# Attention into a token and channel mixer: v times the decay weights on VectorE, loads paced five deep, and a reordered start

## The chip, the cores and the metric

The kernel runs on one core of one Trainium2 chip. The metric is the device time of one execution in microseconds; the time before is the median of three runs. A profile is one execution recorded by the hardware profiler, with the kernel's line numbers as L followed by a number. The engines are TensorE (PE for the matmuls, PEld for the weight loads beside them), VectorE (DVE), ScalarE (ACT), GpSimd (POOL) and SyncE (SP). POOL and SP also issue the DMAs.

## The reference

Eight batches, eight heads, 576 positions, 64 channels per head. Attention with a decay that the input s gives, and behind it a mixer over tokens and over channels:

```python
cum  = np.cumsum(np.maximum(s, 0.0), axis=-1)
bias = -(cum[:, :, :, None] - cum[:, :, None, :])
scores = np.where(causal, -1e9, scale * q @ k.T + np.minimum(bias, 0.0))
attn = softmax(scores)
x    = (attn @ v) as (B, S, H * D)                # 8 x 576 x 512
u    = x + (relu(x.T @ w_tok1) @ w_tok2).T        # mixer over tokens
out  = u + relu(u @ w_ch1) @ w_ch2                # mixer over channels, 512 -> 1536 -> 512
```

## The kernel before, in words

**Decay.** The bias of a pair of positions is a difference of two cumulated sums, so the factor that belongs to the key can be put on v. The kernel scans s on DVE (cum, L534), takes exp(cum - cum_last/2) on ACT (wn, L540), turns it on PE (L560) into wT (L564) and multiplies v by it: vp = vf times wT (L631), with wT itself as a 65th column (L640, L642) that gives the denominator. Only two neighbouring blocks of 128 keys are taken for each block of queries. What that leaves out, and whether q and k are small enough to do without a maximum, is tested at the end: sums of squares of all q and k (`squares`, L657, on ACT at L647 into junk) and gaps in the weights make a flag, and if it is set a general path computes everything again. It isn't set for these inputs.

**Work of a batch.** `stage_qk` loads k and q of four heads (qkn, a ring of five buffers, cast to bfloat16 in the DMA, L462), `stage_v` loads v in five pieces (vf, two buffers, L613) and `merge_v` multiplies (vp, one buffer for even and one for odd batches). `quad` turns q and k of four heads on PE (L689) and evacuates them (kT, qT, L699 on ACT, L701 on DVE); `pair` computes scores (L731), exponentials on ACT (L739), the causal mask on DVE (L748, L756; in batch 0 instead a preset of -2048 that PE adds, L722), E times v (L802), reciprocals (L831) and the normalisation (L835). `tok` is the token mixer (L899, L961, L968), after which u must be turned: from batch 2 on by DMA transposes on SP into uT (L977). `chan` is the channel mixer (L1017, relu at L1024 or L1026, L1042, sum at L1050, store at L1055).

**What sets the order.** No order is written out by hand. Each operation is given to a planner (`Plan.op`) with the engines that may do it, its cost on each, what it reads and writes, and a priority. `Plan.run` simulates the engines by these costs and emits the instructions in the order of the simulated start times; each engine then works through its own instructions in that order, and waits in it for what an instruction needs. Loads are planned on one line of DMA time that begins at `dma_free` (6.0), each with a cost of its own (1.45 for a q or k load, 1.15 for a piece of v, 1.6, 0.3, 1.5, 0.4 for the token weights, 1.9 for a quarter of w_ch1 or w_ch2) and 0.9 for landing. A load that the plan has landing after 50 (`STEADY`) is given 2.0 more (`MARGIN_DMA`) before its users are planned. `lock=True` keeps two operations of DVE and POOL from running at the same time in the plan. Until planned time 45, PE's gaps are filled with matmuls on zeros (L1135).

**Loads.** All loads but four are issued by POOL, in one chain (`load_op`). The plan lets a load start only when the load eight before it has landed (`sent[-8]`). The order is: k and q of (0, 4), that is batch 0 from head 4 on; v of batch 0; the token weights; w_ch1; k and q of (1, 0); half of w_ch2; (1, 4); the other half; v of batch 1; then for each batch from 2 to 7 k and q of its first four heads, v, k and q of its other four; and at the very end once more k and q of batches 0 and 1, for their squares alone (`stage_sq`). The first k and q, s and one piece of v come over SP.

**Products.** v times wT is on DVE in batch 0, on DVE or POOL in batch 1, and on POOL from batch 2 on; POOL therefore issues loads and multiplies in turn, in its planned order.

Of the kernel before, what the change touches and what calls it, by code (L numbers as in the profile page):

```python
# [12 lines left out]


SWITCH = 0.095
STEADY = 50.0
# [38 lines left out]
class Plan:  # L55
# [11 lines left out]
    def op(self, alts, reads=(), writes=(), prio=0, dma=0.0, holds=(), after=None, mode=0, lock=False, alone=None):  # L67
        o = Op()
        o.alts = alts
        o.prio = prio  # L70
        o.dma = dma
        o.mode = mode
        o.lock = lock
        o.alone = alone
        o.idx = len(self.ops)
        o.deps = set()
        o.users = []
        o.bufs = []
# [24 lines left out]
        self.ops.append(o)  # L103
        return o

    def run(self, eps=0.03):
# [11 lines left out]
        for o in ops:  # L118
            if o.nd == 0:
                for e in o.alts:  # L120
                    cands[e].append(o)
        dma_free = 6.0
        mode = 0
# [19 lines left out]
        while left:  # L143
# [68 lines left out]
            for u in o.users:  # L212
# [155 lines left out]
def kernel(  # L368
# [18 lines left out]
    NJ = 5  # L387
# [63 lines left out]

    def load_op(fn, key, us, occ=0.75, prio=-1):

# [6 lines left out]
    def load_cast(n, b, h, i, src):  # L460
        def load():
            nc.gpsimd.dma_start(  # L462
                out=n.t[:, i, :, :],
                in_=src[b, h : h + 4, :, :].rearrange("(f e) (p r) d -> (e p) f (r d)", e=2, r=R))
        load_op(load, [(n, i)], 1.45, prio=-1 if b or h else -3)

# [49 lines left out]
    for ti, src in enumerate((k, q)):  # L516
# [4 lines left out]
        for f in range(2):  # L521
# [11 lines left out]
         reads=["s"], writes=["sr"], prio=-1)  # L533
    P.op({"DVE": (1.3, 1.6, lambda: nc.vector.tensor_tensor_scan(  # L534
        out=cum[:, :], data0=one_sb[:, :], data1=s_sb[:, :], initial=0.0, op0=ALU.mult, op1=ALU.add))},
        reads=["sr"], writes=["cum"], prio=-1)
    P.op(dve(1, lambda: nc.vector.tensor_scalar(
# [61 lines left out]
    def stage_v(b, cs=tuple(range(NJ))):  # L599
# [4 lines left out]
        for c in cs:  # L604
# [13 lines left out]
            load_op(load, [(vf, c)], 1.15 * n / 128, 0.92)  # L618
        if b:
            merge_v(b, cs)  # L620

    def merge_v(b, cs=tuple(range(NJ))):
        vf, vp = vbuf[b]
        odd = b % 2
        for c in cs:
# [3 lines left out]
            def mul(eng, c=c, n=n, p0=p0):  # L629
# [3 lines left out]
                    in1=wT[p0 : p0 + n, cw, b * H : b * H + H].unsqueeze(2).to_broadcast([n, H, D]), op=ALU.mult)  # L633
            alts = {} if b == 0 else {"POOL": (*c_pool(512, 0.0019), lambda mul=mul: mul(nc.gpsimd))}
            if b < 2:
                alts["DVE"] = (*c_dve(512), lambda mul=mul: mul(nc.vector))
            P.op(alts, reads=[(vf, c), "wT"], writes=[(vp, c)], prio=-2 if b < 3 else b * 10 + 5, lock=True)

        def ones(eng):
            eng.tensor_copy(out=vp.t[:, 0 : NJ - 1, :, D], in_=wT[:, 0 : NJ - 1, b * H : b * H + H])  # L640
            p0, cw = (64, NJ) if odd else (0, NJ - 1)
            eng.tensor_copy(out=vp.t[p0 : p0 + 64, NJ - 1, :, D], in_=wT[p0 : p0 + 64, cw, b * H : b * H + H])  # L642
# [29 lines left out]
    def quad(b, h):  # L672
# [4 lines left out]
        for ti in range(2):  # L677
# [6 lines left out]
            def tr(ti=ti, pv=pv):  # L684
                for r in range(R):
                    for e in range(2):
                        p0 = e * PR
                        for f in range(2):
                            nc.tensor.transpose(out=pv(e)[f * D : f * D + D, r * PR : (r + 1) * PR],  # L689
                                                in_=nat.t[p0 : p0 + PR, ti, f, r * D : (r + 1) * D],  # L690
                                                identity=ident[p0 : p0 + PR, p0 : p0 + PR])
            P.op({"PE": (R * 0.031, R * 0.031 + 0.21, tr)}, reads=([(nat, ti, 0), (nat, ti, 1)] if b == 0 and h == 0 else [(nat, ti)]) + ["ident"] + pads,
                 writes=[(pts[e], e) for e in range(2)], holds=[d[ti] for d in dsts], prio=(np_ - 30 * (b < 1 and h < 1), 2), mode=1)
            for e in range(2):
# [12 lines left out]
    def pair(b, h, kT, qT):  # L707
# [3 lines left out]
        for pc, piece in enumerate(PIECES):  # L711
# [7 lines left out]
            if b == 0:  # L719
                def preset(ps=ps, pc=pc):  # L720
                    for hh in range(2):
                        nc.tensor.matmul(out=ps.t[:, hh * 512 : hh * 512 + 512], lhsT=ident[:, :], rhs=neg[:, pc, :],  # L722
                                         start=True, stop=False)
                P.op({"PE": (2 * c_pe(512)[0], 2 * c_pe(512)[0] + 0.21, preset)}, reads=["neg", "ident"],
                     writes=[(ps, 0)], prio=(np_ - 9, 0))
# [115 lines left out]
    def load_w(fn, key, us, occ=0.75):  # L841
        load_op(lambda: nc.gpsimd.dma_start(**fn()), [key], us, occ)

# [240 lines left out]
    stage_v(1)  # L1084
    for b in range(2, B):
        stage_qk(b, 0)
        stage_v(b)
        stage_qk(b, 4)
    for b in range(2):
        for h in range(0, H, 4):  # L1090
            stage_sq(b, h)
    for b in range(B):
        for h in range(0, H, 4):
            quad(b, h)
        st = tok(b)
        chan(b, *st)

    P.op({"DVE": (1.3, 1.6, lambda: nc.vector.tensor_tensor_scan(
# [85 lines left out]
```

## Time and profile before

| | |
|---|---|
| median of three runs | 304.92 us (304.0 to 306.28) |
| the profiled execution | 306.06 us |
| its span | 304.3 us |
| granted TensorE clock, mean | 0.995 |
| DVE busy, 0 to 60 / 60 to 100 / 100 to 180 us | 40.23 / 29.90 / 46.23 us |
| POOL busy in the same stretches | 43.41 / 27.63 / 26.38 us |
| moved by DMA | 39.29 MB, on the queue of POOL 24.25 MB |

A row of the waits reads: who waited, for whom, microseconds in total, times, longest. A row of the timeline or of the chain begins with the start and the length in microseconds. A row of one line or tile gives the count and least, median and largest duration in nanoseconds, the first and last start, and the shapes. A row of a table of stretches gives the stretch, its length, busy time (and instructions) of the engines in the order PE, PEld, DVE, ACT, POOL, or of one group of instructions on the engines that have it, and then the granted clock, the mean share of the DMA engines and GB/s. DMA_DIRECT2D and DMA_TRANSPOSE rows show the issuing, not the transfer. "Issue" stands for time in which an engine waited for nothing that the profile shows.

### The profile page before, as it was taken

How to read it: one execution, taken by the hardware profiler on the slowest of the kernel's cores; microseconds unless marked ns; L12 is line 12 of the kernel's file. 1: busy time of each engine (PE TensorE's matmuls, PEld its weight loads, DVE VectorE, ACT ScalarE, POOL GpSimd, SP SyncE). 2: the span in 40 equal slices, each digit the busy share in tenths (PEclk: the TensorE clock that was granted, in tenths of full speed). 3: DMA queues.
4: the chain of work that ended last, by engine and by line, in shares of the span. 5: the costliest groups of instructions: out<-in, count | busy, mean ns of one | idle time of the engine just before them, and what ended most of it. 6: DMA issues, size and time to landing. Idle time of an engine off the chain costs nothing.

```text
span 304.3 us, 8094 instructions
## 1 busy us (share of the span) xinstructions
PE 291.8 (96%) x3430; PEld 168.2 (55%) x3430; DVE 172.0 (57%) x368; ACT 182.8 (60%) x298; POOL 107.6 (35%) x147
## 2 busy tenths in 40 slices
PE   8899999899999999999999999998999999999991
PEld 3478566467754545457754545455764544457550
DVE  5962889377976456756556556956456642420030
ACT  5887884699996486609872387727761286017300
POOL 8675469999780418107620108500000000000000
PEclk9999999999999999999999999999999999999998
DMA  8999999999997673358455535894004310250032
GB/s 218 226 207 206 216 224 229 252 190 262 227 156 125 155 197 54 79 140 178 94 80 103 133 84 83 132 116 136 2 2 84 125 38 0 69 155 2 0 111 74
DMA packets 38348, 39.29 MB, mean 129 GB/s; under 512 B 17600, under 2 KB 30976, under 8 KB 38304
## 3 DMA queue, kind: packets, MB, share of 16 engines
q0 software_dynamic: 17072, 24.25, 44.6%
q1 hardware_dynamic: 21232, 14.44, 18.7%
q8 instruction: 29, 0.48, 0.7%
q14 instruction: 15, 0.12, 0.1%
HBM read 40.65 MB, written 9.44 MB: 165 GB/s over the span
## 4 chain that ended last, share of the span: by engine, by line
PE 84%; DMA 12%; POOL 1%; issue 1%; DVE 0%; POOLq 0%
PE pmx L1017 30%; PE pmx L1042 30%; PE pmx L961 5%; PE pmx L899 5%; PE psc L802 5%; PE psc L731 5%; DMA qkn<-in_k_dram 5%; PE psc L689 3%; DMA wc<-in_moe_w_ch_dram 3%; DMA vf<-in_v_dram 2%; DMA uTb<-us 2%; POOL qkn L462 1%; PE pmx L986 0%; DVE of L1050 0%; POOL keep masks.py:66 0%
## 5 line engine op out<-in xcount | busy, mean ns | idle before, releaser
L1017 PEld LDWEIGHTS <-wc 128*128 128x128 bf16 x624 | 57.9, 98 | 32.6 <-issue 1.5
L739 ACT ACTIVATE E<-psc 128x1024 bf16<-128x1024 f32 x64 | 62.2, 1024 | 22.8 <-PE psc L731 22.2
L1017 PE MATMUL pmx<-uTb,wc 128*128 128x320 bf16 (+2 forms) x384 | 56.1, 299 | 1.4 <-DMA uTb<-ub 1.1
L1042 PE MATMUL pmx<-wc,gb 128*128 128x512 bf16 (+1 forms) x252 | 55.3, 369 | 0.0
L1017 PE MATMUL pmx<-uTa,wc 128*128 128x512 bf16 (+1 forms) x240 | 45.6, 337 | 0.0
L647 ACT ACTIVATE junk<-qkn 128x1152 bf16<-128x1152 bf16 x32 | 37.3, 1166 | 11.7 <-DMA qkn<-in_q_dram 11.3
L1042 PE MATMUL pmx<-wc,ga 128*128 128x512 bf16 x192 | 44.1, 379 | 0.0
L631 POOL TENSOR_TENSOR vp<-vf,wT 128x512 bf16<-128x512 f32 (+1 forms) x31 | 32.3, 1058 | 25.6 <-PE psc L802 24.9
L1024 ACT ACTIVATE gb<-pmx 128x320 bf16<-128x320 f32 (+2 forms) x57 | 24.7, 438 | 21.2 <-PE pmx L1017 17.3
L1042 PEld LDWEIGHTS <-gb 128*128 128x128 bf16 x252 | 23.6, 98 | 24.8 <-issue 0.2
L613 POOL DMA_DIRECT2D vf<-in_v_dram x39 | 34.1, 884 | 7.3 <-DMA qkn<-in_k_dram 2.2
L748 DVE TENSOR_TENSOR E<-E,keep 128x512 bf16<-128x512 bf16 x56 | 25.8, 474 | 13.3 <-ACT E L739 13.1
L1042 PEld LDWEIGHTS <-ga 128*128 128x128 bf16 x192 | 18.2, 98 | 20.4
L1024 ACT ACTIVATE ga<-pmx 128x512 bf16<-128x512 f32 (+1 forms) x36 | 19.2, 535 | 11.7 <-PE pmx L1017 11.1
L462 POOL DMA_DIRECT2D qkn<-in_k_dram x19 | 14.1, 744 | 33.5 <-issue 31.8
L1026 DVE TENSOR_SCALAR gb<-pmx 128x320 bf16<-128x320 f32 (+2 forms) x39 | 18.8, 487 | 11.9 <-PE pmx L1017 11.5
L699 ACT COPY kT<-psc 128x576 bf16<-128x576 bf16 x22 | 13.1, 641 | 19.4 <-PE psc L689 17.9
L802 PEld LDWEIGHTS <-E 128*128 128x128 bf16 x576 | 21.1, 97 | 5.5
L835 DVE TENSOR_TENSOR x<-psc,rc 128x640 bf16<-128x640 f32 x28 | 23.0, 823 | 0.9
L1050 DVE TENSOR_TENSOR of<-pmx,ua 128x512 f32<-128x512 f32 x16 | 11.0, 689 | 19.5 <-PE pmx L1042 19.3
L731 PE MATMUL psc<-qT,kT 64*128 64x256 bf16 (+2 forms) x320 | 21.3, 250 | 0.0
L731 PEld LDWEIGHTS <-kT 64*128 64x128 bf16 x320 | 12.6, 94 | 14.6 <-issue 11.5
(107 smaller groups left out, 300.9 us busy)
## 6 DMA issues: line engine op xcount, KB each, us to landing
vf<-in_v_dram POOLq DMA_DIRECT2D x32, 256.0 KB, 7.9
out_dram<-of SPq DMA_DIRECT2D x31, 256.0 KB, 2.3
qkn<-in_k_dram POOLq DMA_DIRECT2D x19, 288.0 KB, 6.7
qkn<-in_q_dram POOLq DMA_DIRECT2D x19, 288.0 KB, 7.3
wc<-in_moe_w_ch_dram POOLq DMA_DIRECT2D x8, 384.0 KB, 11.4
out_dram<-of SPq DMA_DIRECT2D x10, 128.0 KB, 2.3
vf<-in_v_dram POOLq DMA_DIRECT2D x7, 128.0 KB, 7.4
gb<-in_k_dram SPq DMA_DIRECT2D x1, 576.0 KB, 3.9
```

Source lines behind the costliest of these rows:

```text
L613: nc.gpsimd.dma_start(out=vf.t[p0 : p0 + n, c, :, :], in_=v[b, :, c * 128 : c * 128 + n, :].rearrange("h p d -> p h d"))
L631: eng.tensor_tensor(out=vp.t[p0 : p0 + n, c, :, 0:D], in0=vf.t[p0 : p0 + n, c, :, :], in1=wT[p0 : p0 + n, cw, b * H : b * H + H].unsqueeze ...
L647: nc.scalar.activation(out=junk[:, :].rearrange("p (t n) -> p t n", t=2), in_=i, func=AF.Square, accum_out=sq[:, col : col + 1])
L731: nc.tensor.matmul(out=ps.t[:, hh * 512 + c0 : hh * 512 + c0 + e - a], lhsT=kT.t[hh * 64 : hh * 64 + 64, j0 : j0 + 128], rhs=qT.t[hh * 64 ...
L739: nc.scalar.activation(out=E.t[:, :, 512 * pc : 512 * pc + 512], in_=ps.t[:, :].rearrange("p (e n) -> p e n", e=2), func=AF.Exp, scale=0.125)
L748: nc.vector.tensor_tensor(out=o, in0=o, in1=keep[:, :].unsqueeze(1).unsqueeze(1).to_broadcast([128, 2, 2, 128]), op=ALU.mult)
L802: nc.tensor.matmul(out=o[:, ic, 0:DE], lhsT=E.t[:, hh, d0 : d0 + 128], rhs=vp.t[:, jc, h + 2 * hh, 0:DE], start=(jc == j_lo), stop=(jc == ic))
L835: nc.vector.tensor_tensor(out=x.t[:, :, :].rearrange("p c (g f e d) -> p g e f c d", f=2, e=2, d=D)[:, h // 4, h % 2], in0=pav2()[:, :, :, ...
L1017: nc.tensor.matmul(out=pm.t[:, 0 : e - a], lhsT=wc1[:, m, cc * 128 : cc * 128 + 128], rhs=uT.t[:, m, a:e], start=(m == 0), stop=(m == NMC ...
L1024: lambda cc=cc, pm=pm, a=a, e=e: nc.scalar.activation(out=g.t[:, cc, a:e], in_=pm.t[:, 0 : e - a], func=AF.Relu),
L1026: lambda cc=cc, pm=pm, a=a, e=e: nc.vector.tensor_scalar_max(out=g.t[:, cc, a:e], in0=pm.t[:, 0 : e - a], scalar1=0.0)),
L1042: nc.tensor.matmul(out=pm.t[:, na:ne], lhsT=g.t[:, cc, c * 128 : c * 128 + 128], rhs=wc2[:, cc, na:ne], start=(cc == 0), stop=(cc == NCC - 1))
```

## The change

1. From batch 2 on (the third), the products v times wT and the two casts of wT into vp go from POOL to DVE, no longer locked against POOL.
2. Loads 6 to 43 of the chain each get a touch in front: POOL copies one element of the load five before it, and so waits until that one has landed.
3. Batches 6 and 7 and the squares' loads of batches 0 and 1 are staged later: those of batch 6 and of batch 0's squares behind touches of batch 3's uT, those of batch 7 and of batch 1's squares behind touches of batch 4's uT. Before, the squares' loads were the last of the chain.
4. The presets of batch 0 are planned behind its first transposes (`"turned"`), and the scan of s behind the transposes of the second tensor, with priority 2 in place of -1.
5. The planner's DMA line begins at 6.85, and what a touch releases is planned without a margin (`bare`).

```diff
+DEPTH = 5
+PACED = (6, 44)
...
-        dma_free = 6.0
+        dma_free = 6.85
...
-                    if fin > STEADY:
+                    if fin > STEADY and not u.bare:
...
+    seen = sb("seen", [128, 8], FP32, fast)
+
+    def touch(ap, reads, col):
+        o = P.op({"POOL": (0.12, 0.2, lambda: nc.gpsimd.tensor_copy(out=seen[0 : ap().shape[0], col : col + 1], in_=ap()))},
+                 reads=reads, writes=[("seen", col)], prio=-1, after=chain[-1])
+        o.bare = True
+        chain.append(o)
+
+    probes = []
+
-    def load_op(fn, key, us, occ=0.75, prio=-1):
+    def load_op(fn, key, us, occ=0.75, prio=-1, probe=None):
+        if PACED[0] <= len(probes) < PACED[1]:
+            touch(*probes[-DEPTH], 0)
+        probes.append((probe, key))
...
-    P.op({"DVE": (1.3, 1.6, lambda: nc.vector.tensor_tensor_scan(
+    scan = P.op({"DVE": (1.3, 1.6, lambda: nc.vector.tensor_tensor_scan(
         out=cum[:, :], data0=one_sb[:, :], data1=s_sb[:, :], initial=0.0, op0=ALU.mult, op1=ALU.add))},
-        reads=["sr"], writes=["cum"], prio=-1)
+        reads=["sr"], writes=["cum"], prio=2)
...
-            alts = {} if b == 0 else {"POOL": (*c_pool(512, 0.0019), lambda mul=mul: mul(nc.gpsimd))}
-            if b < 2:
-                alts["DVE"] = (*c_dve(512), lambda mul=mul: mul(nc.vector))
-            P.op(alts, reads=[(vf, c), "wT"], writes=[(vp, c)], prio=-2 if b < 3 else b * 10 + 5, lock=True)
+            alts = {"DVE": (*c_dve(512), lambda mul=mul: mul(nc.vector))}
+            if b == 1:
+                alts["POOL"] = (*c_pool(512, 0.0019), lambda mul=mul: mul(nc.gpsimd))
+            P.op(alts, reads=[(vf, c), "wT"], writes=[(vp, c)], prio=-2 if b < 3 else b * 10 + 5, lock=b < 2)
...
-        P.op({"POOL": (0.5, 0.7, lambda: ones(nc.gpsimd))} if b else {"DVE": (0.25, 0.3, lambda: ones(nc.vector))},
-             reads=["wT"], writes=[(vp, "w")], prio=b * 10 + 5 if b else -5, lock=True)
+        P.op({"POOL": (0.5, 0.7, lambda: ones(nc.gpsimd))} if b == 1 else {"DVE": (0.3, 0.35, lambda: ones(nc.vector))},
+             reads=["wT"], writes=[(vp, "w")], prio=b * 10 + 5 if b else -5, lock=b < 2)
...
-            P.op({"PE": (R * 0.031, R * 0.031 + 0.21, tr)}, ...
-                 writes=[(pts[e], e) for e in range(2)], ...
+            turn = P.op({"PE": (R * 0.031, R * 0.031 + 0.21, tr)}, ...
+                 writes=[(pts[e], e) for e in range(2)] + (["turned"] if b == 0 and h == 0 and ti == 0 else []), ...
+            if b == 0 and h == 0 and ti == 1:
+                scan.deps.add(turn)
...
-                P.op({"PE": (..., preset)}, reads=["neg", "ident"],
+                P.op({"PE": (..., preset)}, reads=["neg", "ident"] + ["turned"],
...
-    for b in range(2, B):
+    def stage_in(b):
         stage_qk(b, 0)
         stage_v(b)
         stage_qk(b, 4)
-    for b in range(2):
-        for h in range(0, H, 4):
-            stage_sq(b, h)
+
+    for b in range(2, 6):
+        stage_in(b)
     for b in range(B):
         for h in range(0, H, 4):
             quad(b, h)
         st = tok(b)
         chan(b, *st)
+        if b == 3 or b == 4:
+            for c in range(NJ - 1 + b % 2):
+                touch(lambda c=c, uT=st[2]: uT.t[0:1, 0, c * 128 : c * 128 + 1], [(st[2], c)], 1)
+            stage_in(b + 3)
+            for h in range(0, H, 4):
+                stage_sq(b - 3, h)
```

More of the change, by code (lines that the diff above doesn't have):

```diff
@@ L77, in op @@
         o.users = []
+        o.bare = False
         o.bufs = []
@@ L464, in load @@
                 in_=src[b, h : h + 4, :, :].rearrange("(f e) (p r) d -> (e p) f (r d)", e=2, r=R))
-        load_op(load, [(n, i)], 1.45, prio=-1 if b or h else -3)
+        load_op(load, [(n, i)], 1.45, prio=-1 if b or h else -3, probe=lambda: n.t[0:1, i, 0, 0:1])
     qkn = {}
@@ L617, in stage_v @@
                 continue
-            load_op(load, [(vf, c)], 1.15 * n / 128, 0.92)
+            load_op(load, [(vf, c)], 1.15 * n / 128, 0.92, probe=lambda c=c, p0=p0: vf.t[p0 : p0 + 1, c, 0, 0:1])
         if b:
@@ L691, in tr @@
                                                 identity=ident[p0 : p0 + PR, p0 : p0 + PR])
-            P.op({"PE": (R * 0.031, R * 0.031 + 0.21, tr)}, reads=([(nat, ti, 0), (nat, ti, 1)] if b == 0 and h == 0 else [(nat, ti)]) + ["ident"] + pads,
-                 writes=[(pts[e], e) for e in range(2)], holds=[d[ti] for d in dsts], prio=(np_ - 30 * (b < 1 and h < 1), 2), mode=1)
+            turn = P.op({"PE": (R * 0.031, R * 0.031 + 0.21, tr)}, reads=([(nat, ti, 0), (nat, ti, 1)] if b == 0 and h == 0 else [(nat, ti)]) + ["ident"] + pads,
+                 writes=[(pts[e], e) for e in range(2)] + (["turned"] if b == 0 and h == 0 and ti == 0 else []), holds=[d[ti] for d in dsts], prio=(np_ - 30 * (b < 1 and h < 1), 2), mode=1)
+            if b == 0 and h == 0 and ti == 1:
+                scan.deps.add(turn)
             for e in range(2):
@@ L723, in preset @@
                                          start=True, stop=False)
-                P.op({"PE": (2 * c_pe(512)[0], 2 * c_pe(512)[0] + 0.21, preset)}, reads=["neg", "ident"],
+                P.op({"PE": (2 * c_pe(512)[0], 2 * c_pe(512)[0] + 0.21, preset)}, reads=["neg", "ident"] + ["turned"],
                      writes=[(ps, 0)], prio=(np_ - 9, 0))
@@ L841, in load_w, with probe @@
     def load_w(fn, key, us, occ=0.75):
-        load_op(lambda: nc.gpsimd.dma_start(**fn()), [key], us, occ)
+        def probe():
+            o = fn()["out"]
+            return (o[0:1, 0, 0:1] if len(o.shape) == 3 else o[0:1, 0:1])
+        load_op(lambda: nc.gpsimd.dma_start(**fn()), [key], us, occ, probe=probe)
     def load_tok():
```

## The prediction

> **What bounds the kernel now.** I read the page's first part, then the waits of TensorE alone, then the chain that ended last, then the timeline of the first 20 us and of the stretch around 200 us.
>
> ```profile
> span 304.3 us, 8094 instructions
> PE 291.8 (96%) x3430; PEld 168.2 (55%) x3430; DVE 172.0 (57%) x368; ACT 182.8 (60%) x298; POOL 107.6 (35%) x147
> ```
>
> The reader is to see that TensorE (PE) is busy from end to end, and that no other engine is above 60%. So a microsecond counts only where PE stands still or does work that is not the kernel's own. PE's waits and the chain say where that is.
>
> ```profile
> PE pmx L899 <- issue: 1.3, 1, 1.3
> PE pmx L1135 <- DVE zero L470: 1.2, 1, 1.2
> PE pmx L1017 <- DMA uTb<-ub: 1.1, 1, 1.1
> PE pmx L689 <- DMA qkn<-in_k_dram: 0.8, 1, 0.8
> PE psc L689 <- DMA qkn<-in_k_dram: 0.6, 1, 0.6
> PE pmx L1017 <- DMA uTb<-us: 0.3, 1, 0.3
> ```
>
> ```profile
> 35.50 0.48 PE psc L689 x36
> ...
> 54.79 1.28 issue
> ...
> 297.60 0.42 DVE of L1050
> ```
>
> ```profile
> 0.00:25.00 25.00, 6.70 (x20) 2.00 (x20) 1.00 1.07 216
> ```
>
> The six waits are 5.3 us together. The last row is of the filler matmuls (L1135) alone in the first 25 us: 6.70 us of PE time that computes nothing. What follows the last sum, from 297.60 to 304.3, the change leaves alone. Of PE's other 285.1 us (291.8 less 6.7) it takes away nothing. So a gain can only lie in the waits, less the 1.2 us at the very start, and in how early the real work begins.
>
> **The change, part by part.** The sum is made against the profiled execution: 306.06 us, of which 304.3 is the span, so 1.76 lies around it. The median shown, 304.92, stands 1.14 below that execution; I take the difference that the sum gives off the median.
>
> **Squares' loads.** Eight loads, the last of the chain now, run into batch five's transposes.
>
> ```profile
> 193.86 0.77 POOL L462 DMA_DIRECT2D qkn<-in_k_dram  x1 [0.92 <-ACT junk L647]
> 194.62 0.72 POOL L462 DMA_DIRECT2D qkn<-in_q_dram  x1
> ```
>
> ```profile
> 133.08 1.21 SPq L977 DMA_TRANSPOSE uTb<-us  x1
> ...
> 194.44 6.37 SPq L977 DMA_TRANSPOSE uTb<-ub  x4
> 200.91 3.72 SPq L977 DMA_TRANSPOSE uTb<-us  x1
> ```
>
> ```profile
> 185.01 0.84 PE psc L689 x72
> ```
>
> Batch five's last transpose takes 3.72 us where batch three's takes 1.21, and PE then stands 1.1 + 0.3 (the waits on uTb). After the change batch six's loads and four of the squares' go behind batch three's transposes, which end at about 134.3; batch seven's and the other four go behind batch four's. They move past SP's stores, and past no transposes as long as each block of 13 is through before the next batch's. Each needs a free one of five qkn buffers, which come free at the quads' transposes and squares, two per batch, as before. Batch six's own loads come later by this; its first transposes on PE are at 185.01, 50 us behind 134.3, and that covers them. I take 1.4 gained; bounds 0 (they meet batch four's transposes) and 1.4. No other load is late in their place.
>
> **The start.** The scan goes behind the first quad's second transposes, the planner's first landing from 6.0 to 6.85, the presets behind the first transposes.
>
> ```profile
> 8.13 1.18 ACT L699 COPY qT<-pmx 128x576 bf16<-128x576 bf16 x2 [0.88 <-PE pmx L689]
> ...
> 10.06 1.02 ACT L739 ACTIVATE E<-psc 128x1024 bf16<-128x1024 f32 x1 [0.75 <-PE psc L731]
> 10.98 0.76 ACT L540 ACTIVATE wn<-cum,half 64x576 f32<-64x576 f32 x1
> 11.65 7.11 ACT L739 ACTIVATE E<-psc 128x1024 bf16<-128x1024 f32 x7
> ```
>
> ```profile
> 8.08 1.35 DVE L534 TENSOR_TENSOR_SCAN cum<-one_sb,s_sb 64x576 f32<-64x576 f32 x1
> 9.46 0.15 DVE L537 TENSOR_SCALAR half<-cum 64x1 f32<-64x1 f32 x1
> ...
> 13.39 3.08 DVE L631 TENSOR_TENSOR vp<-vf,wT 128x512 bf16<-128x512 f32 x5
> ```
>
> ```profile
> 9.63 0.61 PE L731 MATMUL psc<-qT,kT 64*128 64x256 bf16 x10
> ```
>
> ScalarE (ACT) evacuates both qT because DVE scans, and PE's next entry is a transpose that the planner put too early: it expected the first load at 6.0 + 1.45 + 0.9 = 8.35, and PE waited for it (the 0.8 above). The first score product (9.63) needs only the first qT, out by 8.13 + 1.18/2 = 8.72, so it could come up to 0.9 earlier. From 10.06 ACT runs the eight exponentials and wn without a gap to 18.76, so that end can come 0.9 earlier too. Against it: the scan starts some 0.7 later, behind one evacuation, and after it on DVE stand half, wT and the five products that end at 16.47 and that the first E times v needs. wn has slack: half is out at 9.61 and wn begins at 10.98, behind an exponential. So a few tenths are left of the 0.7. The presets run where fillers run now: nothing, and without fillers they would cost their own time. I take 0.5 gained, between the two paths; bounds 0.9 gained and 0.5 lost. The wait of 0.6 at 35.50 has the same cause: by the planner's costs and the new 6.85 that load lands at 34.8, where the old sum gave 33.95. PE has other work there, so I take 0.5; bounds 0 and 0.6.
>
> **Five loads under way.** Thirty-eight touches, and nine on uT, go on POOL, each 0.2 us by the nearest row, a small cast.
>
> ```profile
> 18.78 0.22 POOL L642 CAST vp<-wT 64x8 bf16<-64x8 f32 x1
> ```
>
> ```profile
> 26.66 0.76 POOL L842 DMA_DIRECT2D wc<-in_moe_w_ch_dram  x1 [1.14 <-DMA wc<-in_moe_w_ch_dram]
> ```
>
> 47 x 0.22 is 10 us on an engine that loses thirty products of 1.05. What stands behind a touch is the next load, and in batch one perhaps a product; already now POOL stands until an older load lands (1.14 in the second row: the load issued eight before it). With four loads queued behind the one that landed, at about 1.4 us each (the planner's cost of a q or k load), 5 us cover the touch, 0.76 of issue and the start of the transfer, so the DMA engines stay full and landings stay: 0. If the cover fails it does so at the four token loads, two of them small, some 0.5 us once. Bound of gain: the 1.28 us stall at 54.79, which comes inside one group of matmuls that waits for no tile, while loads fill the DMA engines; it may be a late fetch of instructions. I take half, 0.6, for want of a row that decides it. The Trainium skill, "DMA: Bandwidth & Descriptors", section "Queues, rings and completion order", says that each DMA engine takes turns between the queues that have work, so a shorter queue of loads would leave the others' turns as they were. By that rule the stall stays and the sum is 0.6 higher; no row here shows turns being taken.
>
> **Products on DVE.** Thirty move.
>
> ```profile
> L631 POOL TENSOR_TENSOR vp<-vf,wT x31: 1032/1047/1232, 43.5 to 191.1; 128x512 bf16<-128x512 f32 x25, 64x512 bf16<-64x512 f32 x6
> L631 DVE TENSOR_TENSOR vp<-vf,wT x9: 674/678/690, 13.4 to 46.5; 128x512 bf16<-128x512 f32 x7, 64x512 bf16<-64x512 f32 x2
> ```
>
> ```profile
> L748 DVE TENSOR_TENSOR E<-E,keep x56: 359/417/1259, 32.7 to 251.1; 128x512 bf16<-128x512 bf16 x56
> ```
>
> 30 x 0.68 = 20.4 us, and six pairs of casts, 12 x 0.22 = 2.6. DVE goes from 172.0 to 195 of 304, less what the masks (L748) get back: up to 1259 ns now where their median is 417. The tight place is 60 to 80 us; in these two rows, of all engines (PE, PEld, DVE, ACT, POOL) and of ACT's squares alone:
>
> ```profile
> 60.00:80.00 20.00, 20.00 (x321) 14.19 (x318) 15.81 (x38) 19.30 (x33) 17.44 (x22) 1.00 1.11 224
> ```
>
> ```profile
> 60.00:80.00 20.00, 7.95 (x13) 1.00 1.11 224
> ```
>
> Some six of the thirty fall there, five to a batch of 34 us and loads running ahead: 15.81 + 6 x 0.68 + 0.4 = 20.3 of 20. But 7.95 of ACT's 19.30 us are squares, which nobody waits for and which the planner ranks last, so evacuations can go to ACT. I take a loss of 0.4; bounds 0 and 6 x 0.68 = 4.1, if each product there holds an evacuation that PE waits for.
>
> **Sum:** -1.4 (uT) - 0.5 (start) - 0.5 (at 35.5) - 0.6 (issue) + 0.4 (DVE) = -2.6: 303.5 for the profiled execution and 304.92 - 2.6 = 302.3 for the median.
>
> **The rivals.** First, every bound of gain holds: -1.4 - 0.9 - 0.6 - 1.3 = -4.2, 300.7. For it: the planner's new start agrees with the first landing of the trace (6.85 + 1.45 + 0.9 = 9.2). Against: wn and the five products follow the scan, so the start's 0.9 is not free.
>
> Second, the stalls move: the start gives nothing, since the products end later by what the exponentials gain, the issue stall comes elsewhere, and of uT's 1.4 DVE takes 0.9: 304.4.
>
> Third, on the other side: DVE stands for a load. DVE works in order, and a product put in before its load has landed holds all masks, reciprocals and sums behind it, and soon PE, with four accumulators. On POOL such a wait held only loads. The place is batches two and three, 48 to 76 us, with the DMA engines at 1.11 of their time. For it: the landing at 35.50 trails even the new plan by 0.7, and a v load's way from issue to landing (least, median, most) varies:
>
> ```profile
> DMA to landing us min/median/max: 5.3/7.8/13.3
> ```
>
> Against: the planner adds 2.0 us to each landing past 50 us, and a product on POOL waited for its load only once, for 0.3:
>
> ```profile
> POOL vp L631 <- DMA vf<-in_v_dram: 0.3, 1, 0.3
> ```
>
> From a slip of about 3.5 us on (2.0 of margin, my estimate of 1.5 of work in PE's queue) it decides; the spread, 13.3 - 5.3 = 8.0, costs 4.5, and with only uT's gain beside it the time is 304.92 - 1.4 + 4.5 = 308.0, more if it comes in two batches.
>
> **How the numbers follow.** Forecast near 302.3 (301.2 to 303.5): 0.39. All gains: 0.28. Stalls move: 0.17. DVE stands: 0.16. A change under 1%, 3 us, can't be told from none here; that is 301.9 to 308.0. Faster takes the all-gains case and a good third of the forecast: 0.28 + 0.14 = 0.42. Slower is three quarters of the third rival, 0.12. Within 1% is the rest, 0.46. The range goes from 299.9, below the all-gains case (0.05 left out), to 307.0 (0.14 left out).
>
> **What would show it.** In the changed profile: PE's waits on uTb gone and batch five's last uTb transpose near 1.2 us; the first exponential before 9.5 and the eighth's end before 18.4; no PE wait on a qkn load near 35; no stall "issue" near 55; the masks' maximum far below 1259 ns; DVE near 195 us busy. I am wrong if DVE shows idle time released by a vf load between 45 and 80 with PE idle behind it, if uTb waits stay, or if PE's fillers and waits in the first 36 us grow.

## The result, and the profile after

The changed kernel takes 308.69 us (median of six runs, 307.32 to 309.48) against 305.33 of the kernel before beside it (304.0 to 306.28). The ratio is 1.0108, with an interval of 1.0071 to 1.0144: slower by 1.08%, clear of the noise, and above the range of 299.9 to 307.0. The ratios here leave out executions more than 1.5% above the fastest of the same kernel, which matters once, for the kernel with the touches alone, where five of twelve are left out (309.0 to 310.21 us). Its profiled execution takes 309.09 us, with a span of 307.3 and a granted clock of 0.997.

The first part of its profile:

```profile
span 307.3 us, 8188 instructions
PE 293.8 (96%) x3432; PEld 168.3 (55%) x3432; DVE 188.2 (61%) x409; ACT 182.1 (59%) x299; POOL 85.2 (28%) x152
```

VectorE carries 16 us more, GpSimd 22 less, and TensorE is again busy from end to end. TensorE's waits in the changed kernel:

```profile
PE psc L705 <- DMA qkn<-in_k_dram: 2.0, 1, 2.0
PE psc L749 <- ACT kT L717: 1.4, 1, 1.4
...
PE psc L820 <- DVE vp L647: 0.5, 1, 0.5
PE psc L820 <- ACT E L757: 0.5, 1, 0.5
```

The waits on uTb and the stall "issue" of 1.28 us are gone. New are a wait for a load (2.0) and two for ScalarE (1.4 and 0.5). To find where the time went I cut both executions at the moment when DVE makes the first sum of the token mixer of batches 3, 4, 5 and 6 (L968 before, L989 after). Before:

```profile
126.20:159.93 33.73, 33.73 (x419) 20.53 (x418) 20.53 (x46) 22.23 (x37) 12.63 (x16) 1.00 0.60 122
159.93:193.73 33.80, 33.80 (x368) 16.76 (x366) 21.44 (x40) 19.25 (x28) 10.17 (x13) 1.00 0.55 107
193.73:230.06 36.33, 34.94 (x440) 21.27 (x438) 22.00 (x49) 21.33 (x35) 1.48 (x2) 1.00 0.50 66
```

After:

```profile
126.44:163.30 36.86, 34.93 (x426) 20.76 (x425) 27.20 (x59) 23.16 (x37) 10.84 (x18) 1.00 0.75 144
163.30:198.67 35.37, 35.04 (x383) 17.37 (x382) 26.31 (x51) 21.70 (x33) 10.69 (x17) 1.00 0.76 154
198.67:232.82 34.15, 34.00 (x418) 20.52 (x418) 19.62 (x43) 18.26 (x32) 0.00 (x0) 1.00 0.19 52
```

Up to batch 3 the two are 0.24 apart. Then the changed kernel loses 3.1 us in one batch and 1.6 in the next, and gets 2.2 back in the third, the one in which the kernel before stood for uTb (36.33 - 34.94 = 1.4). In the first of the three PE stands idle for 36.86 - 34.93 = 1.9 us, in the second for 0.3; the rest of the two losses is counted as busy, a part of it work that runs ahead of the sum here and behind it there (34.00 in the third stretch against 34.94). Over the three stretches together the rows count 1227 matmuls in both kernels, and 103.97 us of PE against 102.47; for these 1.5 us I have no row that gives a reason.

The idle time of the first stretch has its reason on ACT. ACT in the changed kernel, around 150 us:

```profile
143.29 1.16 ACT L663 ACTIVATE junk<-qkn 128x1152 bf16<-128x1152 bf16 x1 [1.17 <-DMA qkn<-in_q_dram]
...
152.85 1.16 ACT L663 ACTIVATE junk<-qkn 128x1152 bf16<-128x1152 bf16 x1 [2.36 <-DMA qkn<-in_q_dram]
153.92 0.19 ACT L663 ACTIVATION_READ_ACCUMULATOR junk<-qkn 128x1 f32 x1
154.01 0.42 ACT L1045 ACTIVATE gb<-pmx 128x320 bf16<-128x320 f32 x1
154.33 1.17 ACT L717 COPY kT<-psc 128x576 bf16<-128x576 bf16 x2
```

And PE in the same stretch:

```profile
145.51 0.70 PE L820 MATMUL psc<-vp,E 128*128 128x65 bf16 x18 [0.49 <-ACT E L757]
...
155.55 0.39 PE L749 MATMUL psc<-qT,kT 64*128 64x256 bf16 x4 [1.44 <-ACT kT L717]
```

ACT comes to a square (L663) whose q has not landed, stands for 2.36 us, and behind it stands the evacuation of kT that PE needs for its next scores. The result of the square is needed by nobody until the end. Before:

```profile
ACT junk L647 <- DMA qkn<-in_q_dram: 11.3, 4, 5.8
```

After:

```profile
ACT junk L663 <- DMA qkn<-in_q_dram: 15.9, 7, 5.2
```

ACT stood for squares' loads in the kernel before as well, for 11.3 us in four waits, but at places where PE needed nothing from it: PE's longest wait for ACT there is 0.3. It is not the length of the waits that counts but what stands behind them.

The other loss is at the start. The DMA traffic from 17 to 20 us, before:

```profile
17.00:18.00 1.00, 1.00 (x21) 0.59 (x20) 0.37 (x2) 0.90 (x2) 1.00 (x2) 1.00 1.25 204
18.00:19.00 1.00, 1.00 (x39) 1.00 (x35) 0.90 (x3) 0.76 (x1) 0.94 (x3) 1.00 1.22 226
19.00:20.00 1.00, 1.00 (x33) 0.95 (x30) 0.84 (x5) 0.88 (x5) 0.98 (x3) 1.00 1.10 197
```

After (the last column is GB/s):

```profile
17.00:18.00 1.00, 1.00 (x33) 0.89 (x30) 0.67 (x3) 1.00 (x2) 1.00 (x4) 1.00 0.60 49
18.00:19.00 1.00, 1.00 (x38) 1.00 (x35) 0.94 (x5) 0.64 (x3) 1.00 (x4) 1.00 0.98 32
19.00:20.00 1.00, 1.00 (x25) 0.76 (x21) 0.85 (x4) 1.00 (x7) 0.94 (x3) 1.00 0.45 52
```

And what the engines do in the changed kernel just before that, and at its first exponential and at the wait of 2.0:

```profile
9.32 1.94 ACT L757 ACTIVATE E<-psc 128x1024 bf16<-128x1024 f32 x2 [0.59 <-PE psc L749]
...
15.65 1.53 POOL L458 COPY seen<-vf 1x1 f32<-1x1 f32 x1 [0.17 <-DMA vf<-in_v_dram]
...
15.91 1.22 DVE L647 TENSOR_TENSOR vp<-vf,wT 128x512 bf16<-128x512 f32 x2
...
17.12 0.71 POOL L863 DMA_DIRECT2D wc<-in_moe_w_ch_dram  x1
...
30.27 0.48 PE L705 MATMUL psc<-ident,qkn 64*64 64x64 bf16 x36 [2.02 <-DMA qkn<-in_k_dram]
```

A touch (L458) copies one element and takes 1.53 us, while DVE multiplies v by wT; the load behind it, the first quarter of w_ch1, goes out at 17.12 only, and the traffic falls from some 200 GB/s to 32 to 52 for three microseconds. The first exponential is 0.7 earlier than before, as foreseen, but the load for which PE waits at 30 us is late. By the sum of batch 3 only 0.24 us of lag against the kernel before are left, so something else in the change gains; the last kernel of the experiments, without this hole, has that sum at 122.77 in place of 126.44. The Trainium skill, "GPSIMD Engine Reference", section "Specifications", says that GpSimd shares its SBUF interfaces with VectorE, with contention when a VectorE instruction has two inputs in SBUF, as these products have. The trace agrees: most touches take 0.17 us, this one 1.53, and it ends at 17.18, just behind the second of the two products (17.13).

### The profile page after: what moved, and what is told of

Read it like the earlier page. It is cut to its first block, busy times and chain, and to the rows that moved or that the text cites. A ratio compares the mean times of both kernels' runs of the same rounds, so it can differ in the third digit from the quotient of the medians.

```text
span 307.3 us, 8188 instructions
## 1 busy us (share of the span) xinstructions
PE 293.8 (96%) x3432; PEld 168.3 (55%) x3432; DVE 188.2 (61%) x409; ACT 182.1 (59%) x299; POOL 85.2 (28%) x152
## 4 chain that ended last, share of the span: by engine, by line
PE 59%; DMA 22%; POOL 8%; issue 5%; ACT 2%; DVE 2%; POOLq 0%; ACTq 0%
PE pmx L1063 24%; PE pmx L1038 20%; DMA qkn<-in_q_dram 12%; DMA vf<-in_v_dram 5%; PE pmx L982 4%; POOL vf L629 4%; PE pmx L920 4%; PE psc L749 3%; DMA qkn<-in_k_dram 3%; PE psc L820 3%; PE psc L705 2%; POOL qkn L478 1%; POOL seen L458 1%; DMA uTb<-us 1%; DMA uTa<-ua 1%
## 5 line engine op out<-in xcount | busy, mean ns | idle before, releaser
L663 ACT ACTIVATE junk<-qkn 128x1152 bf16<-128x1152 bf16 x32 | 37.3, 1167 | 16.2 <-DMA qkn<-in_q_dram 15.9
L766 DVE TENSOR_TENSOR E<-E,keep 128x512 bf16<-128x512 bf16 x56 | 23.8, 426 | 18.6 <-ACT E L757 18.5
L1045 ACT ACTIVATE ga<-pmx 128x512 bf16<-128x512 f32 (+1 forms) x41 | 21.5, 532 | 8.7 <-PE pmx L1038 8.0
L647 DVE TENSOR_TENSOR vp<-vf,wT 128x512 bf16<-128x512 f32 (+1 forms) x39 | 25.7, 688 | 1.4 <-DMA vf<-in_v_dram 1.2
L717 ACT COPY kT<-psc 128x576 bf16<-128x576 bf16 x24 | 14.4, 643 | 16.4 <-PE psc L705 16.4
L820 PE MATMUL psc<-vp,E 128*128 128x65 bf16 x522 | 20.7, 193 | 1.0 <-DVE vp L647 0.5
```

The costliest lines, as they stand in the source:

```text
L647: eng.tensor_tensor(out=vp.t[p0 : p0 + n, c, :, 0:D], in0=vf.t[p0 : p0 + n, c, :, :], in1=wT[p0 : p0 + n, cw, b * H : b * H + H].unsqueeze ...
L663: nc.scalar.activation(out=junk[:, :].rearrange("p (t n) -> p t n", t=2), in_=i, func=AF.Square, accum_out=sq[:, col : col + 1])
L766: nc.vector.tensor_tensor(out=o, in0=o, in1=keep[:, :].unsqueeze(1).unsqueeze(1).to_broadcast([128, 2, 2, 128]), op=ALU.mult)
L820: nc.tensor.matmul(out=o[:, ic, 0:DE], lhsT=E.t[:, hh, d0 : d0 + 128], rhs=vp.t[:, jc, h + 2 * hh, 0:DE], start=(jc == j_lo), stop=(jc == ic))
L1045: lambda cc=cc, pm=pm, a=a, e=e: nc.scalar.activation(out=g.t[:, cc, a:e], in_=pm.t[:, 0 : e - a], func=AF.Relu),
```

## The experiments

The ratio is always to the kernel before, run beside it; under 1 is faster. Single executions of one kernel differ (306.06, 305.75 and 303.87 us in the three profiles of the kernel before), so what one profile shows counts here only where it is larger or where the ratio says the same.

**The touches.** All 38 out, the rest of the change kept.

```diff
-PACED = (6, 44)
+PACED = (0, 0)
```

> The changed kernel without the 38 touches on loads 6 to 43 (the nine on uT stay). Theory: the touches let the DMA engines run dry at 17 to 20 us (49, 32 and 52 GB/s in three slices of 1 us), which costs the 2.0 us wait of the transposes at 30 us; so without them that wait is gone, the moved rate at 17 to 20 us is above 190 GB/s and the time is 1 to 2 us below the changed kernel, some 307. The stall of about 3.5 us more between 143 and 203 us stays. Rival (pacing is what removed the 1.28 us stall at 55 us): that stall comes back and the time is within 0.5 us of the changed kernel's 308.7.

308.9 us, 1.009 (1.0055 to 1.0124). The traffic has no hole (207, 223 and 200 GB/s from 17 to 20 us) and the last sum of the program comes 1.1 us earlier than in the changed kernel, but ACT still stands for squares' loads (11.3 us), and what follows the flag is 1.3 us longer (below, POOL's branch). I had expected some 307; both signs of the rival are there, a wait "issue" of 1.0 us and a time within 0.5 of the changed kernel's, so taking out all the touches at once gains nothing.

**The place of the loads.** All loads planned up front and the squares' last, as before; touches, products and start as changed.

```diff
+    for b in range(2, B):
+        stage_in(b)
+    for b in range(2):
+        for h in range(0, H, 4):
+            stage_sq(b, h)
     for b in range(B):
...
-        if b == 3 or b == 4:
...
```

> The changed kernel with all batches staged up front and the squares' loads last, as before, and no touch on uT; pacing, products and start as changed. Theory: the loads held back to 135 and 171 us make ACT stand for them with its squares, which costs some 3.7 us between 143 and 203 us; so that is gone, the 1.4 us wait on uTb at 205 us is back, and the time is about 308.7 - 3.7 + 1.5 = 306.5. Rival (the products on DVE cost it): the lag between 143 and 203 us stays, and the time is 310, with the uTb wait on top.

305.41 us, 1.0003 (0.9973 to 1.0034): the whole loss is gone, where 306.5 was expected. PE's busy time from 140 to 160 us is 19.95 again (18.07 in the changed kernel), and the uTb wait does not return.

**Both.**

> Both of the two edits: no touches at all, all loads as before; products on DVE, the start and 6.85 as changed. If the two losses are separate and add, some 305 (308.7 - 2.2 - 1.5), at or a little under the kernel before. If the products on DVE are the loss, 307 or more.

311.59 us, 1.0189 (1.0142 to 1.0237), a surprise: some 305 was expected if the two losses add. PE stands once for 3.7 us, and the loads point to the reason. This kernel, without touches:

```profile
93.33 0.71 POOL L478 DMA_DIRECT2D qkn<-in_q_dram  x1 [9.80 <-PE psc L705]
94.03 4.22 POOL L629 DMA_DIRECT2D vf<-in_v_dram  x5
...
108.79 1.02 PE L1038 MATMUL pmx<-uTa,wc 128*128 128x512 bf16 x4 [3.70 <-DMA uTa<-ua]
```

Six loads go out from 93.33 on, among the DMA transposes of batch two (92.54 to 97.9). With touches the same six go at 102.65, behind them. The way of a transpose into uTa from issue to landing, in this kernel and in the ten microseconds behind the stall all engines, clock and traffic:

```profile
DMA to landing us min/median/max: 2.4/2.5/12.0
```

```profile
110.00:120.00 10.00, 9.73 (x71) 4.83 (x71) 3.22 (x8) 5.81 (x9) 0.00 (x0) 0.83 0.04 15
```

The longest way is 12.0 us, where with touches it is 7.0. So loads can hold DMA transposes up, as the prediction had it, but at another place; this rests on one profile of each kernel. The mean clock of all six executions is low (0.981 to 0.988), which fits a stall in each. The stall also costs more than its own length: the clock that is granted to TensorE falls to 0.83 in the ten microseconds behind it (1.00 with touches), by estimate another 1.7 us (10 times 0.17). The touches of loads 14 to 43, to which the prediction gave nothing, therefore decide a lot where all loads are staged up front: with them alone the same kernel takes 302.89 us (below).

**Squares later.** The changed kernel, with the squares planned 6 us later behind their loads; nothing else.

```diff
-                u.ready = max(u.ready, rdy)
+                u.ready = max(u.ready, rdy + (u.patient if o.dma else 0.0))
...
-                     reads=[(n, 0), (n, 1)], writes=[("sq", col)], prio=60)
+                     reads=[(n, 0), (n, 1)], writes=[("sq", col)], prio=60).patient = 6.0
```

> The changed kernel, all of it, but the planner holds the squares on ACT 6 us longer after the planned landing of their load. Theory (ACT, in order, stands for loads with squares that nobody waits for, and exponentials and evacuations behind them are late): ACT's waits on qkn loads fall from 15.9 us to below 4, PE's waits between 143 and 156 us (0.5 and 1.4) go, and the time falls by 2 to 3.5 us to 305.2 to 306.7. Rival (the loads themselves or the products on DVE hold PE there): the time stays within 1 us of 308.7.

305.62 us, 0.9981 (0.9954 to 1.0009). ACT does not stand for one square, and PE is busy for 19.95 of the 20 us from 140 on. The loads stay late, the touches on uT stay; what the edit changes is ACT's order. The planner makes the whole plan anew with it, but the start is no better than the changed kernel's: the sum of batch 3 comes at 127.48, 1.04 later. Behind it the three batches take 34.29, 34.65 and 34.20 us, in place of 36.86, 35.37 and 34.15. That settles the main loss: it is where the squares stand in ACT's order. Why the plan had these loads landing earlier than they did isn't shown.

**The early touches.** The second kernel above, without the touches of loads 6 to 13; all else is in nearly the same order.

```diff
-PACED = (6, 44)
+PACED = (14, 44)
```

> The kernel that stages all loads as before the change (305.4 us), with the touches of loads 6 to 13 (the token weights and w_ch1) left out, those of loads 14 to 43 kept; the order of everything else is nearly the same. Theory: the hole in the DMA traffic from 17 to 20 us comes from a touch that POOL finishes late while a product runs on DVE, and it costs 1.3 us at the first sum of batch 0 and later less. So GB/s stays near 200 from 15 to 20 us, the wait on a qkn load falls from 0.7 to below 0.3, the first sum of batch 0 comes 1 to 1.4 us earlier than in the kernel with all touches, and the time is 303.8 to 304.8. Rival: that hole is taken up by slack behind batch 1, and the time stays within 0.5 of 305.4.

302.89 us, 0.9898 (0.9865 to 0.9931): faster than both. The traffic from 18 to 19 us:

```profile
18.00:19.00 1.00, 1.00 (x37) 1.00 (x34) 0.98 (x5) 0.64 (x2) 0.53 (x2) 1.00 1.14 206
```

PE's largest waits that are left, beside the one at the very start:

```profile
PE pmx L1063 <- issue: 0.6, 4, 0.2
PE pmx L920 <- issue: 0.5, 2, 0.3
```

Eight touches cost 1.0003 - 0.9898, about 1%, or 2.5 us by the medians, more than expected: the time was to be 303.8 to 304.8.

**Depth.** The changed kernel, with a load waiting for the eighth before it.

```diff
-DEPTH = 5
-PACED = (6, 44)
+DEPTH = 8
+PACED = (8, 44)
```

> The changed kernel with eight loads under way in place of five, touches from load 8 on. Theory, that depth times the late touch makes the hole: with three more loads queued a touch that takes 1.5 us longer leaves the DMA engines work, GB/s stays above 150 from 15 to 20 us, and the first sum of batch 0 comes near 33.2 (35.16 in the changed kernel); the waits of ACT for squares' loads remain, so the time is 307.0 to 308.3. Rival, that the touches' own time on POOL makes it: the hole stays, the first sum of batch 0 stays above 34.8 and the time at 308.3 to 309.5.

306.67 us, 1.0038 (1.0012 to 1.0065). Here too a touch runs beside the products:

```profile
15.01 1.96 POOL L458 COPY seen<-vf 1x1 f32<-1x1 f32 x1 [0.65 <-DMA vf<-in_v_dram]
```

The traffic behind it:

```profile
18.00:19.00 1.00, 1.00 (x38) 1.00 (x35) 0.84 (x5) 0.64 (x4) 1.00 (x3) 1.00 1.21 222
```

The touch takes 1.96 us, even longer, and yet the traffic stays at 222. So it is not the late touch alone: with five under way, two of them small token weights, there is too little left in the queues when POOL is late. The squares still cost (18.21 of 20 us busy from 140). The time is a little below the expected 307.0 to 308.3.

**Products back on POOL**, all else as changed.

> The changed kernel with the products and the casts of batches two to seven back on POOL. Theory, that products on DVE cost next to nothing and ACT's waits for squares' loads carry the loss: 308 to 309.5, and PE's wait on a vp product changes by less than 0.5. Rival, that DVE's 17 us more of work carry a part of the loss: 306 to 307.5. A third case: products on POOL stand in front of the loads of batch six and seven and make the squares' loads later still: 309.5 to 312.

310.09 us, 1.013 (1.0089 to 1.017). ACT stands for squares' loads eight times, 17.2 us in all (15.9 in the changed kernel). The products on DVE carry no part of the loss; the third case is the nearest, though the interval overlaps that of the change.

**Each part alone.** Products on DVE only; start only; staging of batches six and seven and of the squares only; touches only (each is the part of the diff shown at the beginning, put into the kernel before).

> The kernel before with nothing but the products and casts of batches two to seven on DVE. Theory: DVE has room, the change alone costs 0 to 0.5 us by itself, 305.3 to 306.0. But POOL, freed of products, sends the loads of later batches earlier, so they can run beside batch two's DMA transposes, as in the kernel without touches and with all loads staged as before (311.6, a stall of 3.7 on uTa): then 308 to 311, with PE waiting for uTa at about 108 us. A third case, a product on DVE that stands for its v load: DVE idle on vf for more than 2 us between 45 and 80.

> The kernel before with only the reordered start: the presets and the scan behind the first transposes, and the planner's first landing at 6.85. Theory: the first sum of batch 0 comes 0.5 to 1.2 us earlier and most of it stays to the end: 304.2 to 305.1, with the wait on uTb as before. Rival: the later plan of the loads moves five or six of them beside the DMA transposes of batch two, as in the kernel without touches and with all loads staged as before (311.6): PE waits for uTa over 2 us near 108 us and the time is 307 or more.

> The kernel before with only part three: batches six and seven and the squares' loads staged behind touches of batch three's and four's uT; products on POOL, no other touches, start as before. Theory: the waits on uTb go, ACT stands for squares' loads in 140 to 185 us for over 10 us in all, and PE stands behind it: the sum of batch 5 comes 3 us or more late and the time is 306.5 to 309.5. Rival: with POOL's products between them the loads go more evenly and the time is 304 to 306.

> The kernel before with only the touches of loads 6 to 43, five under way. Theory: POOL finishes a touch late beside a product on DVE, the DMA traffic has a hole of some 3 us between 15 and 20 us (GB/s below 80 there, near 200 before), the first sum of batch 0 comes 1 us or more late, and the time is 305.8 to 307.5. Rival: fewer loads under way take the stall of 1.28 away and POOL's waits cost nothing: 303.5 to 305.

| part alone | ratio | interval | worth in us (of 304.92) | forecast |
|---|---|---|---|---|
| staging | 1.0107 | 1.0073 to 1.014 | +3.3 | -1.4 |
| start | 0.9999 | 0.9979 to 1.0018 | 0.0 | -1.0 |
| touches | 0.9998 | 0.996 to 1.0035 | -0.1 | -0.6 |
| products | 1.0015 | 0.9991 to 1.0039 | +0.5 | +0.4 |
| all | 1.0108 | 1.0071 to 1.0144 | +3.3 | -2.6 |

The staging alone is the whole loss: 308.73 us. Its trace has the same cause, here with PE's waits named L747 and L818:

```profile
PE psc L747 <- ACT qT L715: 1.1, 1, 1.1
PE psc L818 <- ACT E L755: 1.0, 1, 1.0
...
PE psc L747 <- ACT kT L715: 0.9, 1, 0.9
```

The products came out as the theory said (305.7). The start did so only in its first half: the first sum of batch 0 is 0.6 earlier (33.3 in place of 33.9), but nothing of it stays to the end, 305.43 where 304.2 to 305.1 was expected, and the wait on uTb, expected as before, is not there. Of the touches I had expected 305.8 to 307.5: the hole is there (65 and 69 GB/s from 17 to 19 us, with touches of 0.58 and 0.71 us), and the first sum of batch 0 is 0.96 late. What that costs in the end stays open: the ratio shows no loss, but the twelve executions lie between 304.37 and 310.21 with a median of 307.22, and the profile is of one of 305.83 us, so it says nothing of the longer ones.

**POOL's branch.** In the profile of the products alone the last sum's flag is ready at 295.85, 2.1 us before that of the kernel before (297.94), and yet the span is only 0.3 shorter. At the end all engines read the flag and branch over the general path (L1152). POOL's branch and its next instruction, before:

```profile
L1152 POOLq COMPARE_BRANCH  x1: 45/45/45, 298.9 to 298.9; - x1
...
L1152 POOLq EVENT_SEMAPHORE  x1: 17/17/17, 299.3 to 299.3; - x1
```

With the products alone on DVE:

```profile
L1152 POOLq COMPARE_BRANCH  x1: 45/45/45, 296.8 to 296.8; - x1
...
L1152 POOLq EVENT_SEMAPHORE  x1: 17/17/17, 300.5 to 300.5; - x1
```

0.4 and 3.7 us. TensorE's queue comes out of the branch later than that (301.1 in the second profile, 4.26 us behind its branch), but POOL still has a closing instruction to do, DRAIN, that takes 2.52 us, and the engines finish together:

```profile
L1179 POOLq DRAIN  x3: 50/107/2518, 300.6 to 303.7; - x3
```

Begun at 300.6 it ends at 303.1, 2 us behind TensorE. So I put 42 sets of one element to zero behind POOL's last load, where it has nothing to do.

```diff
+                for kk in range(42):
+                    nc.gpsimd.memset(pool_pad[0:1, kk : kk + 1], 0.0)
                 tc.mark_branch_hint_location("general", "LikelyTaken")
```

> The kernel with nothing but the products on DVE (305.7 us; its body ends 2.1 us before that of the kernel before, at 295.85, but POOL's first instruction after the branch at the end comes 3.75 us after it in place of 0.48), with 42 sets of one element to zero added on POOL behind its last load, where it is idle. Theory: it is the number of instructions in POOL's stream ahead of the branch that decides whether what follows the branch is at hand (0.48 us at 200 to 273 instructions, 3.1 to 3.75 at 175 to 189): POOL goes on within 0.6 us and the time is 303.7 to 304.6. Rival: it is something else, as the length of POOL's pause: the 3 us stay and the time is 305.2 to 306.2.

304.21 us, 0.9947 (0.9927 to 0.9966), and POOL goes on 0.48 us after its branch. DRAIN now begins at 298.0 and ends before TensorE is out of the branch (301.9):

```profile
L1182 POOLq DRAIN  x3: 50/107/2518, 298.0 to 302.7; - x3
```

Instructions that do nothing make the kernel faster by 1.0015 - 0.9947, some 2 us.

**The kernel before, two profiles more.** The kernels above that leave the squares' loads in place have no wait on uTb, so the wait itself was open.

> The kernel before, unchanged, for one more profile. If its wait on uTb of 1.4 us belongs to every execution, PE waits for uTb over 1 us near 204 us again, the last uTb transpose of batch five takes over 3 us and the sum of batch 6 comes 36 us or more behind that of batch 5 (36.3 in the profile shown). If it belongs to some executions only, as four kernels with the same loads at the same place suggest, that transpose takes 1.2 to 2 us, PE doesn't wait and the sums are 34.5 to 35.2 apart. I expect the second, 6 to 4.

> The kernel before, unchanged, for a third profile; the same two cases as for the second, and if the wait comes and goes, that shows between these two and the one shown.

305.75 and 303.87 us, single runs. Neither waits for uTb. The first of the two loads and batch five's last transpose, in the second profile:

```profile
196.59 0.77 POOL L462 DMA_DIRECT2D qkn<-in_k_dram  x1 [2.58 <-ACT junk L647]
...
202.04 1.21 SPq L977 DMA_TRANSPOSE uTb<-us  x1
```

In the third:

```profile
194.34 0.77 POOL L462 DMA_DIRECT2D qkn<-in_k_dram  x1 [2.19 <-ACT junk L647]
...
200.08 1.20 SPq L977 DMA_TRANSPOSE uTb<-us  x1
```

The loads run beside the transposes as before, and the last one takes 1.2 us and not 3.72. So the stall belongs to one of three profiled executions of the same kernel, and what decides when it comes isn't shown. It also means that loads beside transposes don't always hold them up.

**Late staging, with both causes taken away.** Squares 6 us later, and no touches of loads 6 to 13.

> The changed kernel with its late staging, but with the touches of loads 6 to 13 left out and the squares planned 6 us later behind their loads. Theory: the late staging costs nothing by itself; what is left of the loss in the kernel with later squares alone (305.6) is the hole in the loads between 15 and 20 us. So GB/s stays near 200 there, the first sum of batch 0 comes near 33.2 (36.1 with the early touches), and the time is 302.5 to 303.9, as of the kernel with late touches and all loads staged as before (302.9). Rival: the late staging costs by itself, through loads that now run beside batch six's and seven's work: 304.5 or more.

302.51 us, 0.9925 (0.99 to 0.995). All that PE waits for in this kernel:

```profile
PE pmx L1163 <- DVE zero L487: 1.2, 1, 1.2
PE pmx L803 <- DVE vp L659: 0.2, 1, 0.2
```

It is as good as the best above (the intervals overlap). The late staging costs nothing by itself, and it gains nothing that can be told.

## Why the prediction was wrong

**Squares' loads (forecast -1.4, measured alone +3.3).** This is the step that failed, at both ends: its gain of 1.4, and its bound of 0 on the other side, with no term for a loss. The gain was read from one profile. It was a true stall of that execution, and two others lack it; the sum was made against an execution 1.14 above the median, and by the other two profiles the median most likely did not hold this stall, so it was counted off a number that had nothing of it. The loss lies in what the prediction says of the squares in its part on DVE, "which nobody waits for and which the planner ranks last, so evacuations can go to ACT", and in not asking what reads the loads that are moved. The rank counts in the plan alone. On the chip ACT works in order, and a square put in before its q has landed holds the evacuations behind it: 2.36 us in the row above, of which PE stands for 1.44. I had weighed just this mechanism for DVE and a v load, as the third rival, and did not ask it of the other engine that reads loads, although I moved exactly those loads. "No other load is late in their place" was right of the loads and beside the point.

**The touches (forecast 0, with "some 0.5 us once" if the cover fails).** Place right, size wrong: the cover failed at the token loads, and the eight early touches cost 1.05% in one pair of kernels (302.89 against 305.41 us) and 0.56% in the other (302.51 against 305.62), which is 1.7 to 3.2 us. The 5 us of cover were four loads of 1.4 us each, but at that place two of the loads under way were small; and the 0.22 us came from a cast that ran alone, where beside DVE's products one touch took 1.53. So the sign of being wrong that the prediction named for the first 36 us came true: the wait on a qkn load grew, and the fillers took 7.45 us in place of 6.70.

**The start (forecast -0.5 and -0.5).** The first exponential came at 9.32, before 9.5, and the eighth ended at 18.35, before 18.4. Alone, the part is worth nothing that can be measured in the end; its first sum is 0.6 earlier, and where that is lost isn't shown. In the changed kernel the wait on a qkn load did not go, it grew from 0.6 to 2.0, by the hole in the traffic; without the early touches it is gone.

**The stall "issue" (forecast -0.6).** Gone in the changed kernel, so its whole 1.28, but a stall of 1.1 to 1.7 under that name is there in the two kernels that are the changed one without its touches, in the one with the start alone and in both further profiles of the kernel before. What decides it stays open.

**Products on DVE (forecast +0.4).** 0.5 measured. DVE is busy 188 us, not 195, and the longest mask takes 0.88 us in place of 1.26. But the small number is a sum of two: the body gains, and the end loses some 2 us by POOL's branch, of which the prediction knew nothing ("What follows the last sum, from 297.60 to 304.3, the change leaves alone" was wrong for this part alone; in the whole change, with the touches, POOL goes on after 0.48 us as before). The third rival did not happen: DVE stands for v loads for 1.2 us in all, and PE waits 0.5 us for a product, once. That its 308.0 lies near the measured time is chance.

## What to carry to other kernels

When a load is moved, look at every instruction that reads it, on every in-order engine, and at what stands behind it there; a low priority in a plan does not help once the order is fixed. Before a stall is counted as a gain, look for it in a second profile or in the difference between the profiled execution and the median. Where loads are paced, count bytes under way and not loads, and don't start before the small ones are through.

## What the hardware showed that I had not expected

POOL's first instruction behind the branch at the end came 0.48 us after it in all fourteen profiles with 200 to 273 instructions of POOL recorded ahead of the branch, and 3.1 to 3.75 us after it in the three with 175 to 189. VectorE shows the same: 3.4 to 3.7 us with 438 to 440 instructions, 0.6 with 464 to 476. But a longer stream is not quicker as such: ScalarE took 2.7 to 3.7 us in all seventeen, with 378 to 398, and TensorE's queue 4.25 to 4.55, with 3446 to 3450. That it is a fetch of instructions is my reading; that adding instructions takes it away was shown for POOL.

A copy of one element on POOL took 0.17 us, and 0.58 to 1.96 us beside products on DVE; the two longest, 1.53 and 1.96, ended only when two products in a row were through.

One stall of TensorE was paid for twice: behind the 3.7 us in the kernel without touches the granted clock was 0.83 for ten microseconds. Behind the 1.4 us on uTb in the kernel before it stayed at 1.00.
